# Layer 2 of a decode kernel: K and V in two places instead of three from unit 3 on, weights in the third, loop from unit 6

## The chip, the cores and the metric

The kernel runs on one core of a Trainium2 chip. The metric is the device time of one execution in microseconds.

## The reference

Two layers with the same weights. Each is an attention over a cache of 16384 keys for 2 batches and 32 heads, followed by a small MLP. There is one query row per batch.

```python
q = (x @ wq)                                              # x: (2, 1, 576), bf16
scores = einsum("bhqd,bhkd->bhqk", q, k_cache) * Dh**-0.5 # caches: (2, 32, 16384, 128)
o = einsum("bhqk,bhkd->bhqd", softmax(scores), v_cache)
x = x + o @ wo                                            # wo: (4096, 576)
...                                                       # mixer and MLP: w2, w3 (576 x 4608), w4 (4608 x 576)
```

The caches are 4 MB for each K and each V of one (batch, head). The kernel calls such a pair a *unit*; a layer has 64. Nearly all of K and V is read from memory twice, once per layer. That is about 1.1 GB, and it is the whole cost.

## The kernel before

A scheduler written in Python records operations with what they read and write, and derives the semaphore waits. One large buffer in SBUF, the memory on the chip, has three *places*, each with room for one K and one V. A queue of wishes says which tile goes where and in which order; a transfer is issued when everything that lies under its target has been read for the last time. The order of the queue is fixed: a tile that can't go yet holds up all behind it.

```python
def place(self, kind, l, i):              # l: layer (0, 1), i: unit in the layer
    if l == 0:
        return i % 2
    if kind == "K":
        return (0, 1, 2)[i % 3] if i < self.ROT else (2, 0)[i % 2]      # ROT = 8
    return (0, 1, 2)[i % 3] if i < self.ROT - 1 else (0, 2)[i % 2]

# in plan(): the order of the transfers in layer 2 (l = 1) is K2 V2 K3 V3 ... K6 V6 K7 K8 V7 wo K9 V8 ...
for l in range(2):
    wp = 2 - l                            # the place of this layer's weights: 2, then 1
    wo_at = wp * self.place_n + unit
    for i in range(U):
        kv("K", l, i, {(1, 2): (2, 1, 1), (1, 3): (2, 2)}.get((l, i)))  # split into several transfers
        ...
    want_w34(l, wp, 2)
```

Layer 1 uses places 0 and 1 for K and V and place 2 for weights. Its last two units are kept, so layer 2 starts with units 0 and 1 in SBUF, and with unit 2 as soon as the MLP has finished with place 2.

TensorE transposes 9 blocks of 16 of a unit's K and multiplies them by the query; VectorE does the other 7 blocks. TensorE then weighs V by the softmax. In the first units of layer 2 ("early") the weighing of the unit before is done in the middle of a unit, so that its V comes free sooner:

```python
first = (2, self.ROT)[l]                  # units from here on are one loop body of two units
self.s.loops.append((l * U + first, (U - first) // 2, 2, ...))
for i in range(U):
    early = l == 1 and 1 <= i < first
    for c in range(ncp):
        self.turn(l, i, c)                # TensorE transposes block c of K; ScalarE copies it
        ...
        if early and c == 4:
            self.weigh(l, i - 1, 0)
            self.weigh(l, i - 1, 1)       # V of unit i-1 is free from here on
    self.release("K", l, self.order[l][i], 1)
    if not early: ...                     # weigh at the end of the unit
```

I write K5 for the K of unit 5 of layer 2, and so on. All of this is about layer 2.

Of the kernel before, what the change touches and what calls it, by code (L numbers as in the profile page):

```python
# [278 lines left out]
class Decode:  # L279
# [3 lines left out]
    N_KEEP = 2  # L283
    N_MID = 3
    EARLY = 7
    ROT = 8
    WO_PIECE = 4
    FJ = 3
    W4_PIECES = ((1, 2, 3, 3, 2, 1), (5, 4, 2, 1))
# [89 lines left out]
        return ap[:, t * 128:(t + 1) * 128] if t < self.KT - 1 else ap[:, self.D - 128:self.D]  # L379


    def place(self, kind, l, i):


        if l == 0:
            return i % 2
        if kind == "K":
            return (0, 1, 2)[i % 3] if i < self.ROT else (2, 0)[i % 2]
        return (0, 1, 2)[i % 3] if i < self.ROT - 1 else (0, 2)[i % 2]

    def plan(self):
        ring, B, H, D, KT, U = self.ring, self.B, self.H, self.D, self.KT, self.U
        unit = 2 * self.half


        heads = [[*range(4, H), 0, 1, 2, 3], [*range(3, H - 1), 0, 1, 2, H - 1]]
        self.order = [[h * B + b for h in o for b in range(B)] for o in heads]
        x = self.order[0][0]
        assert self.order[1][:3] == [*self.order[0][-2:], x]
        self.kept = {(kind, u, h) for kind in "KV" for u in self.order[0][-2:] for h in range(2)} | {("V", x, 1)}  # L400

        def kv(kind, l, i, split=None):
            u = self.order[l][i]
            if l == 1 and (kind, u, 0) in self.kept:
                return
            b, hh = u % B, u // B
            src = {"K": self.K, "V": self.V}[kind][b, hh]
            pl = self.place(kind, l, i)
            at = pl * self.place_n + {"K": 0, "V": unit}[kind]
            ap = src.rearrange("(p j) d -> p (j d)", p=128)  # L410
            if split:
                a, quarter = 0, self.half // 2
                for k, n in enumerate(split):
                    if (kind, u) == ("V", x) and k == 1:
                        if l == 1:
                            continue
                        at = 2 * self.place_n + unit
                    part = ap[:, a * quarter:(a + n) * quarter]
                    ring.want([(kind, l, u, k)], at + a * quarter, n * quarter,
                              [lambda e, v, part=part: e.dma_start(v, part)])  # L420
                    a += n
            else:
                ring.want([(kind, l, u, h) for h in range(2)], at, unit, [lambda e, v: e.dma_start(v, ap)],
                          sem=f"{kind}{pl}")

        def rows(kind, l, w, ats):

            n = w.shape[1]
            for k in range(KT):
                if k < KT - 1:  # L430
                    ap, m = w[k * 128:(k + 1) * 128, :], n
                else:
                    m = n // 2
                    ap = w[k * 128:D, :].rearrange("r (c n) -> (r c) n", c=2)
                ring.want([(kind, l, k)], ats[k], m, [lambda e, v, ap=ap: e.dma_start(v, ap)])  # L435

        def want_w34(l, p, p1):
            base = p * self.place_n
            rows("w3", l, self.w3, [base + k * self.F for k in range(KT)])
            at, a0 = base + (2 * KT - 1) * self.F // 2, 0  # L440
            for c, n in enumerate(self.W4_PIECES[l]):
                m = n * self.FJ * D
                if c == 1:
                    assert at <= mid_at[l]
                    at = p1 * self.place_n
                ap = self.w4[a0 * 128 * self.FJ:(a0 + n) * 128 * self.FJ, :].rearrange(
                    "(a p j) n -> p a (j n)", p=128, j=self.FJ)
                ring.want([("w4", l, c)], at, m,
                          [lambda e, v, ap=ap, n=n: e.dma_start(v.rearrange("p (a m) -> p a m", a=n), ap)])
                at, a0 = at + m, a0 + n  # L450

        def want_w2(at):
            n = 128 * (KT - 1)
            w2a, w2b = self.w2[0:n, :].rearrange("(p r) n -> p (r n)", p=128), self.w2[n:D, :]
            ring.want([("w2",)], at, KT * D, [lambda e, v: e.dma_start(v[:, 0:(KT - 1) * D], w2a),
                                              lambda e, v: e.dma_start(v[0:64, (KT - 1) * D:KT * D], w2b)])

        def want_wo(l, j, at):
            h0, h1 = self.wo_piece(l, j)
            rows = self.wo[h0 * 128:h1 * 128, :]  # L460
            ap = rows.rearrange("(p j) n -> p j n", p=128) if j < self.n_wo else rows.rearrange("(j p) n -> p j n", p=128)
            ring.want([("wo", l, j)], at, (h1 - h0) * D,
                      [lambda e, v: e.dma_start(v.rearrange("p (j n) -> p j n", n=D), ap)],
                      sem="wo" if j < self.n_wo else None)

        n, third = self.wq.shape[1], 2 * self.place_n
        mid_at = [third + unit + self.half - self.N_MID * D, third - self.N_MID * D]
        rows("wq", 0, self.wq, [third + k * n for k in range(KT)])
        for l in range(2):
            wp = 2 - l  # L470
            wo_at = wp * self.place_n + unit
            for i in range(U):
                kv("K", l, i, {(1, 2): (2, 1, 1), (1, 3): (2, 2)}.get((l, i)))
                j = i if l == 1 and i < self.EARLY else i - 1
                if j >= 0 and (j != i - 1 or (l, j) != (1, self.EARLY - 1)):
                    kv("V", l, j, {(0, 0): (2, 2), (1, 2): (2, 2)}.get((l, j)))
                if i % 8 == 0 and 8 <= i <= 8 * self.n_wo:
                    want_wo(l, i // 8 - 1, wo_at)
                if i == 8 * self.n_wo + 2:
                    want_wo(l, self.n_wo, mid_at[l])  # L480
                if l == 0 and i == 0:
                    want_w2(wo_at + n // 2)
            kv("V", l, U - 1, (2, 1, 1))
            want_w34(l, wp, 2)
            if l == 0:
                free = third + (self.FA - self.W4_PIECES[0][0]) * self.FJ * D
                assert free + n <= third + unit + self.half
                rows("wq", 1, self.wq, [free, *(third + k * n for k in range(KT - 1))])
# [464 lines left out]
    def attention(self, l):  # L953
# [3 lines left out]
        self.query_rows(l, 0)  # L957
        first = (2, self.ROT)[l]
        self.s.loops.append((l * U + first, (U - first) // 2, 2, self.WO_PIECE, (9 - first) // 2 % self.WO_PIECE))
# [83 lines left out]
```

## Time and profile before

| | before |
|---|---|
| time | 2564.07 us (2563.78 to 2564.38, three runs) |
| span of the profiled run | 2562.7 us |
| data queue | 1095.66 MB, 99.7% of the span of 16 DMA engines |
| TensorE, VectorE, ScalarE busy | 65%, 68%, 48% |
| instruction packets of 16 KB | 40 |

In the lines of the profile PE is TensorE, PEld its weight loads, DVE VectorE, ACT ScalarE, POOL GpSimd, and SPq the queue of SyncE, which issues the transfers; L423 is line 423 of the kernel. From the page of the kernel before: the mean busy share of the DMA engines in 40 slices (9 is 90% or more), what they moved in each, and the queues (packets, MB, share of 16 engines).

```profile
...
DMA  9999999999999999999999999999999999999998
GB/s 409 430 431 433 431 430 433 432 431 432 430 433 432 431 432 431 433 431 431 426 408 431 428 432 430 432 433 431 432 432 430 432 431 431 433 432 431 430 433 341
...
q1 hardware_dynamic: 46888, 1095.66, 99.7%
q8 instruction: 40, 0.66, 0.1%
...
```

The queue is full in every slice but the last. The weaker slices are the first (409 GB/s), the two around the change of layers (426 and 408) and the last (341). The Trainium skill, page "DMA: Bandwidth & Descriptors", section Specifications, states a fabric ceiling of 435 GB/s, and the trace agrees: 428 to 433 in the slices between.

From the table of stretches of the kernel before (from and to in us from the span's start, length, busy us and count on each engine, then granted clock of TensorE, DMA share and GB/s):

```profile
...
core 0: us, PE busy (x) PEld busy (x) DVE busy (x) ACT busy (x) POOL busy (x), PEclk, DMA share, GB/s
...
1364.00:1368.00 4.00, 2.97 (x50) 2.98 (x51) 3.69 (x6) 1.51 (x2) 0.00 (x0) 0.50 1.01 434
1368.00:1372.00 4.00, 3.19 (x64) 2.95 (x62) 3.63 (x7) 3.31 (x6) 0.00 (x0) 0.91 0.94 397
1372.00:1378.00 6.00, 5.09 (x145) 4.55 (x144) 5.58 (x7) 4.79 (x9) 0.00 (x0) 1.00 1.03 436
1378.00:1384.00 6.00, 5.42 (x105) 5.42 (x105) 5.89 (x9) 3.41 (x5) 0.00 (x0) 0.58 1.02 434
1500.00:2480.00 980.00, 625.92 (x13949) 580.46 (x13946) 679.65 (x986) 474.27 (x750) 0.00 (x0) 0.67 1.00 431
...
```

In the stretch from 1364 to 1384 us the queue is full (0.94 to 1.03; a packet is counted whole in the stretch in which it starts, so a short stretch can show more than 1).

From the DMA queue's issues of the kernel before (start, length, line, target and source). They are V4, K5, V5 and K6:

```profile
...
start us, us, engine line op out<-in xcount [idle before <-releaser]
1347.50 0.33 SPq L423 DMA_DIRECT2D buf<-in_A_v_cache_dram  x1
1353.76 0.33 SPq L423 DMA_DIRECT2D buf<-in_A_k_cache_dram  x1
1365.57 0.33 SPq L423 DMA_DIRECT2D buf<-in_A_v_cache_dram  x1
1370.11 0.33 SPq L423 DMA_DIRECT2D buf<-in_A_k_cache_dram  x1
...
```

And what the DMA queue waited for between 1340 and 1385 us in the kernel before (L179 is the scheduler's own wait instruction, here for VectorE's reading of a K):

```profile
...
engine line waited for: us in total, times, longest us
SPq L423 <- PE ops L870: 29.4, 3, 11.5
SPq L179 <- DVE prod L827: 14.0, 3, 5.4
SPq L423 <- PE sps L815: 0.7, 1, 0.7
```

K5 goes at 1353.76 and V5 at 1365.57 us. When those transfers start matters less than when the one ahead has landed. Each of the 16 DMA engines reports its own landing; this is read from the trace's landing records:

| before | first engine | last engine | lag of the last |
|---|---|---|---|
| first half of K2 | 1316.5 | 1317.6 | 1.0 |
| V4 | 1365.3 | 1368.3 | 3.0 |
| K5 | 1375.0 | 1378.4 | 3.3 |
| V5 | 1384.7 | 1388.0 | 3.2 |
| V9 and all later ones of the loop | 1473.5 | 1479.7 | 6.2 |

A full tile of 4 MB takes 9.7 us. K5 was issued 11.5 us before V4's first engine had finished, V5 9.4 us before K5's: the queue has slack. And the slowest engine falls behind the fastest while unrolled code runs (until 1474 us), and then no more.

### The profile page before, as it was taken

The page shows a single profiled execution, that of the slowest core. Times are in us where ns is not written, and L with a number is a line of the kernel's source. Part 1 is how long each engine was busy: PE and PEld are TensorE (multiplying, and loading weights), DVE is VectorE, ACT ScalarE, POOL GpSimd, SP SyncE. Part 2 cuts the span into 40 slices and gives each one's busy share as a digit, 9 for nine tenths or more (in the row PEclk, how much of TensorE's full clock was granted, in tenths as well). Part 3 has the DMA queues.
Part 4 walks back from the last instruction along what each step waited for, and adds up shares of the span by engine and source line. Part 5 has one row for each costly group of instructions (what it writes and reads, how often), then busy time and mean ns, then how long its engine had stood idle before and what let it go on. Part 6 is the DMA issues. An engine that isn't in the chain of part 4 may idle for free.

```text
span 2562.7 us, 84020 instructions
## 1 busy us (share of the span) xinstructions
PE 1671.5 (65%) x36847; PEld 1559.0 (61%) x36847; DVE 1751.6 (68%) x2595; ACT 1231.3 (48%) x1944; POOL 1.0 (0%) x12
## 2 busy tenths in 40 slices
PE   5666666666666656666688766666656666665666
PEld 5555665565565656655678765565656555565566
DVE  5676767677666766766648777666767766676674
ACT  4544544454445445544446554454445544544452
POOL 0000000000000000000000000000000000000000
PEclk8666666666666666766666666666666666666665
DMA  9999999999999999999999999999999999999998
GB/s 409 430 431 433 431 430 433 432 431 432 430 433 432 431 432 431 433 431 431 426 408 431 428 432 430 432 433 431 432 432 430 432 431 431 433 432 431 430 433 341
DMA packets 46936, 1096.38 MB, mean 428 GB/s; under 512 B 4964, under 2 KB 6056, under 8 KB 11560
## 3 DMA queue, kind: packets, MB, share of 16 engines
q1 hardware_dynamic: 46888, 1095.66, 99.7%
q8 instruction: 40, 0.66, 0.1%
q14 instruction: 8, 0.07, 0.0%
HBM read 1095.64 MB, written 0.00 MB: 428 GB/s over the span
## 4 chain that ended last, share of the span: by engine, by line
DMA 59%; issue 16%; DVE 13%; PE 10%; ACT 1%; SPq 0%; DVEq 0%
DMA buf<-in_A_k_cache_dram 56%; DVE prod L827 11%; PE tps L798 6%; DMA buf<-in_B_w_dram 1%; DVE sd L830 1%; PE misc L846 1%; DMA buf<-in_A_v_cache_dram 1%; PE ops L870 1%; ACT ktsb L802 1%; PE misc L693 1%; DMA buf<-in_A_wq_dram 0%; PE sps L815 0%; SPq L435 0%; PE sps L655 0%; ACT p L856 0%
## 5 line engine op out<-in xcount | busy, mean ns | idle before, releaser
L802 ACT ACTIVATE ktsb<-tps 128x1024 bf16<-128x1024 bf16 x1155 | 1124.2, 1031 | 871.2 <-PE tps L798 866.2
L798 PE MATMUL tps<-ident,buf 128*128 128x128 bf16 x9240 | 911.7, 263 | 616.5 <-DMA buf<-in_A_k_cache_dram 600.4
L798 PEld LDWEIGHTS tps<-ident,buf 128*128 128x128 bf16 x9240 | 735.0, 120 | 643.1 <-DMA buf<-in_A_k_cache_dram 619.7
L830 DVE TENSOR_REDUCE sd<-prod 128x8 f32<-128x1024 bf16 x893 | 1089.5, 1220 | 31.0
L827 DVE TENSOR_TENSOR prod<-buf,qb 128x1024 bf16<-128x1024 bf16 x893 | 608.6, 682 | 11.4 <-DMA buf<-in_A_k_cache_dram 10.5
L870 PE MATMUL ops<-p,buf 128*128 128x1 bf16 x16384 | 461.7, 164 | 66.5 <-DMA buf<-in_A_v_cache_dram 57.4
L870 PEld LDWEIGHTS ops<-p,buf 128*128 128x128 bf16 x16384 | 443.7, 100 | 76.4 <-DMA buf<-in_A_v_cache_dram 66.4
L848 DVE TENSOR_REDUCE small<-misc 128x1 f32<-128x128 f32 x128 | 37.3, 292 | 635.8 <-PE misc L846 635.8
L815 PE MATMUL sps<-qcur,ktsb 128*128 128x1 bf16 x9240 | 396.8, 166 | 109.0 <-ACT ktsb L802 88.2
L815 PEld LDWEIGHTS sps<-qcur,ktsb 128*128 128x128 bf16 x9240 | 348.4, 101 | 172.2 <-ACT ktsb L802 166.1
L781 ACT ACTIVATE qb<-misc 128x128 bf16<-128x128 f32 x130 | 36.0, 277 | 369.2 <-PE misc L778 369.2
L846 PE MATMUL misc<-identS,small 128*128 128x128 f32 x256 | 94.4, 472 | 5.2 <-DVE small L840 5.2
L846 PEld LDWEIGHTS misc<-identS,small 128*128 128x128 f32 x256 | 69.7, 332 | 5.8 <-DVE small L840 5.7
L856 ACT ACTIVATE p<-sps,small 128x72 bf16<-128x72 f32 x128 | 41.4, 324 | 6.8 <-DVE small L848 6.8
L856 ACT ACTIVATE p<-sd,small 128x56 bf16<-128x56 f32 x128 | 44.6, 349 | 0.0
L773 ACT ACTIVATE qcur<-qt 128x1 bf16 (+1 forms) x130 | 29.4, 226 | 16.8 <-DVE qt L703 16.8
L778 PE MATMUL misc<-ident,qcur 128*128 128x128 bf16 x130 | 34.6, 266 | 1.3 <-ACT qcur L773 1.3
L925 PE MATMUL misc<-lpiece,small 128*128 128x16 f32 x28 | 8.5, 385 | 41.0 <-DVE lpiece L923 41.0
L925 PEld LDWEIGHTS misc<-lpiece,small 128*128 128x128 f32 x28 | 7.0, 311 | 43.6 <-DVE lpiece L923 43.6
L836 DVE TENSOR_REDUCE small<-sps 128x1 f32<-128x72 f32 x128 | 28.5, 223 | 4.1 <-PE sps L815 4.1
L693 PE MATMUL misc<-prod,buf 128*128 128x2 bf16 (+1 forms) x360 | 24.6, 179 | 6.6 <-DMA buf<-in_B_w_dram 4.6
L693 PEld LDWEIGHTS misc<-prod,buf 128*128 128x128 bf16 (+1 forms) x360 | 22.4, 111 | 8.8 <-issue 4.7
(94 smaller groups left out, 270.8 us busy)
## 6 DMA issues: line engine op xcount, KB each, us to landing
buf<-in_A_k_cache_dram SPq DMA_DIRECT2D x124, 4096.0 KB, 24.3
buf<-in_A_v_cache_dram SPq DMA_DIRECT2D x122, 4096.0 KB, 33.6
buf<-in_A_v_cache_dram SPq DMA_DIRECT2D x5, 2048.0 KB, 22.5
buf<-in_B_w_dram SPq DMA_DIRECT2D x8, 1152.0 KB, 30.7
buf<-in_A_wq_dram SPq DMA_DIRECT2D x8, 1024.0 KB, 9.0
buf<-in_A_wo_dram SPq DMA_DIRECT2D x14, 576.0 KB, 34.6
buf<-in_A_k_cache_dram SPq DMA_DIRECT2D x3, 2048.0 KB, 11.2
buf<-in_A_v_cache_dram SPq DMA_DIRECT2D x4, 1024.0 KB, 23.8
```

The lines of the kernel that those rows point to most:

```text
L693: ins = pe.matmul(out[lo:128, t * self.B:(t + 1) * self.B], lhsT=w[:, t * 128:(t + 1) * 128 - lo], rhs=rhs, start=(first and t == 0), stop ...
L778: self.pe(lambda pe: pe.matmul(self.misc[:, 0:128], lhsT=bcast(self.qcur[:, q:q + 1], 128), rhs=self.ident[:, :], start=True, stop=True), ...
L781: self.act(lambda a: a.activation(out=self.qb[q][:, :], in_=self.misc[:, 0:128], func=ACT.Copy), r=["P:misc"], w=[f"qb{q}"])
L798: ins = pe.transpose(self.tps[b][:, j * 128:(j + 1) * 128], kt[:, (j0 + j) * 128:(j0 + j + 1) * 128], self.ident[:, :])
L802: self.act(lambda a: a.activation(out=self.ktsb[k][:, :, :].rearrange("p a b -> p (a b)"), in_=self.tps[b][:, :], func=ACT.Copy), r=[f"P:t ...
L815: ins = pe.matmul(self.sps[sp][:, col:col + 1], lhsT=self.ktsb[k][:, j, :], rhs=self.qcur[:, sp:sp + 1], start=True, stop=True)
L827: self.dve(lambda v: v.tensor_tensor(out=self.prod[d][:, :, :], in0=k3, in1=bcast_mid(self.qb[q][:, :], self.CH), op=ALU.mult), r=[*res, f ...
L830: self.dve(lambda v: v.tensor_reduce(out=self.sd[q][:, o:o + self.CH], in_=self.prod[d][:, :, :], axis=AX.X, op=ALU.add), r=[f"prod{d}"], ...
L846: self.pe(lambda pe: pe.matmul(self.misc[:, 128:256], lhsT=bcast(self.m[:, q:q + 1], 128), rhs=self.identS[:, :], start=True, stop=True), ...
L848: self.dve(lambda v: v.tensor_reduce(out=self.bias[:, q:q + 1], in_=self.misc[:, 128:256], axis=AX.X, op=ALU.max, negate=True), r=["P:misc ...
L856: self.act(lambda a, u, c0=c0, c1=c1, src=src: a.activation(out=self.p[q][:, c0:c1], in_=src, func=ACT.Exp, bias=self.bias[:, q:q + 1], sc ...
L870: ins = pe.matmul(self.ops[q][:, 0:1], lhsT=vt[:, j * 128:(j + 1) * 128], rhs=self.p[q][:, h * self.TB + j:h * self.TB + j + 1], start=(h ...
```

## The change

It gives up the third place for K and V after unit 2, so that weights can lie there in both layers, and with the shorter pattern the loop of layer 2 can start at unit 6 instead of 8, which is less code. K5 is split in two halves so that its first half can go as soon as K3's first half is free.

```diff
-    ROT = 8
+    ROT = 6
...
-    def place(self, kind, l, i):
-        if l == 0:
-            return i % 2
-        if kind == "K":
-            return (0, 1, 2)[i % 3] if i < self.ROT else (2, 0)[i % 2]
-        return (0, 1, 2)[i % 3] if i < self.ROT - 1 else (0, 2)[i % 2]
+    def place(self, l, i):
+        if l == 0 or i < 3:
+            return i % 2 if l == 0 else i
+        return (i + 1) % 2
...
         for l in range(2):
-            wp = 2 - l
-            wo_at = wp * self.place_n + unit
+            wo_at = third + unit
             for i in range(U):
-                kv("K", l, i, {(1, 2): (2, 1, 1), (1, 3): (2, 2)}.get((l, i)))
+                kv("K", l, i, {(1, 2): (2, 1, 1), (1, 3): (2, 2), (1, 5): (2, 2)}.get((l, i)))
...
-            want_w34(l, wp, 2)
+            want_w34(l, 2, 2 - l)
```

The cut parts only rename the argument of `place` and move the address of a weight tile.

More of the change, by code (lines that the diff above doesn't have):

```diff
@@ L407, in kv @@
             src = {"K": self.K, "V": self.V}[kind][b, hh]
-            pl = self.place(kind, l, i)
+            pl = self.place(l, i)
             at = pl * self.place_n + {"K": 0, "V": unit}[kind]
@@ L466, in plan @@
         n, third = self.wq.shape[1], 2 * self.place_n
-        mid_at = [third + unit + self.half - self.N_MID * D, third - self.N_MID * D]
+        mid_at = [third + unit + self.half - self.N_MID * D, third + self.place_n - self.N_MID * D]
         rows("wq", 0, self.wq, [third + k * n for k in range(KT)])
         for l in range(2):
-            wp = 2 - l
-            wo_at = wp * self.place_n + unit
+            wo_at = third + unit
             for i in range(U):
-                kv("K", l, i, {(1, 2): (2, 1, 1), (1, 3): (2, 2)}.get((l, i)))
+                kv("K", l, i, {(1, 2): (2, 1, 1), (1, 3): (2, 2), (1, 5): (2, 2)}.get((l, i)))
                 j = i if l == 1 and i < self.EARLY else i - 1
```

## The prediction

> **What bounds it now.** The transfers. The page's DMA line is full in every slice but the last; one queue takes 99.7% of the 16 engines' span for 1095.66 MB. The stretch table gives 431 GB/s in both layers' loops. The Trainium skill ("DMA: Bandwidth & Descriptors", Specifications) gives a fabric ceiling of 435 GB/s; the trace agrees with it and not with that table's 358 GB/s per core. PE (65%) and DVE (68%) have slack: in the loop PE waits some 5.7 us per unit for K. So only bubbles in the transfers, and what the slowest of the 16 engines loses, can move the time.
>
> **What the change does.** Layer 1, layer 2's first units, all bytes, the steady loop (two places in both kernels) and the end stay. Between about 1310 and 1480 us three things move.
>
> 1. In layer 2, K5 waits for unit 3 instead of unit 2, V5 for V3 instead of V2, and so on: one place less of prefetch while compute catches up after the MLP. K5 is split; its first half waits only for the first half of K3.
> 2. Units 6 and 7 move from unrolled code into the loop, so V5 and V6 come free later in their units.
> 3. Two unrolled units less code. The trace has some 23 instruction fetches of 16 KB between 1313 and 1474 us, two per unrolled unit, about 1 us each on one DMA engine. Meanwhile the gap between the first and the last engine's landing of one tile grows from 1.0 to 6.2 us, and stays there.
>
> **Costed from the landings and issues.** V4 lands from 1365.3 (first engine) to 1368.3 us (last). Before, K5 was issued at 1353.8, V5 at 1365.6: no bubble. Now K5's first half can go only when unit 3's eighth block of transposes is done, about 1368.5; at layer 2's first K the first packet came 0.96 us after issue, and first packets took about 1.1 us instead of 0.61. So the queue runs dry: about 1.9 us lost on the slowest engine, 4.9 on the fastest. K5 then lands about 1380; V5 goes at 1379.6 (V3 done): another 1.2 us. K6 (free 1384.5), V6 (1393.6), K7 (1399.8), K8 (about 1416) go before the queue empties. Sum +3.1 us, all critical, since transfers bound the kernel to its end.
>
> In return, four or five fetches fewer: the slowest engine lost 2.9 us to them from 1388 to 1480; I estimate 1 us saved. PE, ACT and DVE work is the same and off the path.
>
> **Prediction:** 2564.1 + 3.1 - 1.0 = about 2566.2 us, 8 in 10 between 2562.8 and 2569.0. Faster by over 2%: 0.003; within 2%: 0.99; slower by over 2%: 0.007.
>
> **What would show it right.** Stretch table: a new dip of DMA share at about 1366 to 1371, a small one at 1380 to 1382; V5 landing 2 to 3 us later than 1388.0; the loop still at 431 GB/s; the same 8 us from the last landing to the end. The DMA queue's waits: K5's first half on PE's transposes, V5 on PE's weighting. Some four instruction packets fewer (40 before), and a gap between first and last landing in the loop below 6.2 us.
>
> **What would make it wrong.** If K5's first half goes before V4 has drained, no bubble, and the saved fetches win: about 2563. If the loop's first pass (units 6, 7) is slow, K8 and K9 slip and more bubbles appear: 2569 or more. If the slow engine's lag is not what ends the kernel, the cost is nearer the 4.9 us of the fast ones.

## The result and the profile after

The changed kernel took 2567.89 us (median of 2565.89, 2566.49, 2569.29 and 2569.38) against 2563.93 us of the kernel before in the same rounds. The ratio is 1.0015, with a 95% interval of 0.9998 to 1.0032: the same at 2%. A ratio is the mean time of one kernel's runs over that of the other's of the same rounds, so it is not quite the ratio of the medians. The first repetition below gave 1.0019 (1.0005 to 1.0033). Over all nine runs the changed kernel has a mean of 2568.2 us, 4.3 us above the 2563.9 us of before. Its runs lie 4.0 us apart, those of before 1.5.

The profile is that of the fastest run (2565.89 us, span 2564.1 us). The same lines of its page:

```profile
...
DMA  9999999999999999999999999999999999999998
GB/s 410 432 428 433 432 432 430 432 433 431 431 431 430 432 433 429 433 433 432 424 411 404 431 431 431 432 431 432 430 431 431 432 430 433 431 431 432 430 432 351
...
q1 hardware_dynamic: 47032, 1095.66, 99.6%
q8 instruction: 35, 0.57, 0.1%
...
```

Slice 22 (of 64 us each, so from 1346 us on) has 404 instead of 431 GB/s, and there are 35 instruction packets instead of 40. The bytes are the same.

The same stretches of the changed kernel:

```profile
...
core 0: us, PE busy (x) PEld busy (x) DVE busy (x) ACT busy (x) POOL busy (x), PEclk, DMA share, GB/s
...
1364.00:1368.00 4.00, 3.74 (x68) 3.56 (x65) 3.93 (x7) 3.59 (x5) 0.00 (x0) 0.66 0.46 135
1368.00:1372.00 4.00, 3.03 (x44) 2.80 (x45) 3.04 (x7) 2.67 (x5) 0.00 (x0) 0.77 0.89 377
1372.00:1378.00 6.00, 6.00 (x174) 6.00 (x172) 5.86 (x8) 3.45 (x7) 0.00 (x0) 0.78 0.97 408
1378.00:1384.00 6.00, 4.81 (x91) 4.46 (x88) 5.89 (x8) 5.07 (x7) 0.00 (x0) 0.80 1.04 401
1500.00:2480.00 980.00, 627.84 (x13954) 583.39 (x13954) 679.54 (x985) 474.44 (x749) 0.00 (x0) 0.67 1.00 431
...
```

Between 1364 and 1368 us the DMA share falls from 1.01 to 0.46, and at 1378 to 1384 the rate falls from 434 to 401 GB/s. The loop (last row) is unchanged. So are TensorE's and VectorE's work; before, they were as busy as now.

The same issues (V4, then the two halves of K5 in one row, V5, K6):

```profile
...
1346.07 0.33 SPq L421 DMA_DIRECT2D buf<-in_A_v_cache_dram  x1
1366.49 2.44 SPq L418 DMA_DIRECT2D buf<-in_A_k_cache_dram  x2
1377.32 0.33 SPq L421 DMA_DIRECT2D buf<-in_A_v_cache_dram  x1
1383.28 0.33 SPq L421 DMA_DIRECT2D buf<-in_A_k_cache_dram  x1
...
```

And the same waits of the DMA queue. The wait of 20.3 us is that of K5's first half, which by the program is for unit 3's eighth block of transposes; the profile puts it down to the matmuls (`sps`) among which that block is issued. `ops` is the weighing of V, where V5 waits for V3:

```profile
...
SPq L418 <- PE sps L812: 20.3, 1, 20.3
SPq L421 <- PE ops L867: 17.2, 2, 8.8
...
```

K5 went 12.7 us later than before, and V5 11.8 us later. V4 had landed at 1364.9 (first engine) to 1367.4 us (last), so the queue ran dry. V5 landed at 1390.7 instead of 1388.0 us. In the loop the lag of the slowest engine is 3.2 us instead of 6.2. The last transfer landed at 2555.9 us, 1.4 us later than before, and from there to the end the kernels take 8.1 and 8.2 us.

### The profile page after: what moved, and what is told of

It reads as the page before. It is cut to its first block, busy times and chain, and to the rows that moved or that the text cites. A ratio compares the mean times of both kernels' runs of the same rounds, so it can differ in the third digit from the quotient of the medians.

```text
span 2564.1 us, 84103 instructions
## 1 busy us (share of the span) xinstructions
PE 1663.0 (65%) x36847; PEld 1544.4 (60%) x36847; DVE 1751.5 (68%) x2595; ACT 1228.4 (48%) x1944; POOL 1.0 (0%) x12
## 4 chain that ended last, share of the span: by engine, by line
DMA 59%; issue 16%; DVE 15%; PE 8%; ACT 1%; SPq 0%; DVEq 0%
DMA buf<-in_A_k_cache_dram 56%; DVE prod L824 12%; PE tps L795 5%; DVE sd L827 2%; DMA buf<-in_B_w_dram 2%; PE misc L843 1%; DMA buf<-in_A_v_cache_dram 1%; PE misc L690 1%; ACT ktsb L799 1%; PE ops L867 1%; DMA buf<-in_A_wq_dram 0%; SPq L433 0%; DVE small L845 0%; PE sps L652 0%; PE sps L812 0%
## 5 line engine op out<-in xcount | busy, mean ns | idle before, releaser
L795 PE MATMUL tps<-ident,buf 128*128 128x128 bf16 x9240 | 896.1, 260 | 621.4 <-DMA buf<-in_A_k_cache_dram 605.5
L795 PEld LDWEIGHTS tps<-ident,buf 128*128 128x128 bf16 x9240 | 722.1, 119 | 647.4 <-DMA buf<-in_A_k_cache_dram 625.0
```

The lines of the kernel that those rows point to most:

```text
L795: ins = pe.transpose(self.tps[b][:, j * 128:(j + 1) * 128], kt[:, (j0 + j) * 128:(j0 + j + 1) * 128], self.ident[:, :])
```

## The experiments

Two theories were put against each other. *The hole*: K5 and V5 wait for a unit more, the queue runs dry, and a kernel that is bound by transfers never gets that back, except for what the saved instruction fetches return. *The loop*: units 6 and 7 moved into the loop free their V later and start with a cold first pass, and that is what costs. All runs gave the right result. Each was timed in five rounds beside the kernel before, whose median was between 2563.90 and 2564.01 us in each of the three sets. The sets ran on three chips; since before is equal on them, medians of different sets are compared here.

### The changed kernel again

No edit.

> The changed kernel again, unedited, to see whether its two groups of times (2565.9 and 2566.5; 2569.3 and 2569.4 us) come back. Theory (the bubble at K5 and V5 plus the fetches that are saved): times between 2565.5 and 2570 us, in two groups or spread; if this profile is of a long run (2569 us), K5's first half is issued later than the 1366.5 us of the first profile, by 2 to 3 us, or the lag of the slowest engine in the loop is above 3.2 us; which of the two tells where the 3 us lie. Rival (the loop's first pass over units 6 and 7 costs the time): the bubble is the same in both groups and K8 or K9 comes late instead.

Measured: 2568.4 us (2567.31 to 2569.87), ratio 1.0019 (1.0005 to 1.0033). The two groups did not come back; the times are spread. The profiled run took 2568.40 us. Its K5 (both halves) and V5:

```profile
...
1368.35 1.86 SPq L418 DMA_DIRECT2D buf<-in_A_k_cache_dram  x2
1379.21 0.33 SPq L421 DMA_DIRECT2D buf<-in_A_v_cache_dram  x1
...
```

and its stretches:

```profile
...
1364.00:1368.00 4.00, 3.20 (x52) 3.20 (x53) 3.90 (x7) 1.74 (x2) 0.00 (x0) 0.50 0.19 78
1368.00:1372.00 4.00, 3.20 (x64) 2.95 (x63) 3.44 (x6) 3.31 (x6) 0.00 (x0) 0.94 0.69 233
...
```

K5 went 1.9 us later than in the first profile of the same kernel, V5 too, and the run was 2.5 us longer. The hole is deeper: a DMA share of 0.19 from 1364 to 1368 us. So in these two profiles the longer run is the one with the longer hole, and compute was through unit 3 later in it by as much: unit 4's query comes at 1370.6 instead of 1368.7 us. That the other runs differ for the same reason is likely but not shown, as they were not profiled.

### The loop put back to unit 8

```diff
 # the changed kernel
-    ROT = 6
+    ROT = 8
```

> The changed kernel with the loop put back to unit 8 (units 6 and 7 unrolled and early again); the two places stay. Theory: the bubble stays (K5 and V5 wait as in the changed kernel), the fetches come back (about 40 packets), so it is slower than the changed kernel by about 1 us: 2567 to 2570.5 us. Rival (the earlier loop is what costs): as fast as before, 2564 us, since the loop is undone.

Measured: 2569.69 us (2568.79 to 2570.35), ratio 1.0023 (1.0009 to 1.0036), 40 instruction packets. The loop is undone and the time is 1.3 us longer than in the repetition, not 4.5 us shorter. The theory of the loop falls.

### Three places up to unit 5, loop from unit 6

```diff
 # the kernel before
-    ROT = 8
+    ROT = 6
 ...
-        if kind == "K":
-            return (0, 1, 2)[i % 3] if i < self.ROT else (2, 0)[i % 2]
-        return (0, 1, 2)[i % 3] if i < self.ROT - 1 else (0, 2)[i % 2]
+        return i % 3 if i < self.ROT else (0, 2)[i % 2]
 ...
-            want_w34(l, wp, 2)
+            want_w34(l, wp, (2, 0)[l])
```

> Three places up to unit 5 as in the kernel before (so K5 waits for unit 2 again, V5 for V2), two places after, loop from unit 6 as in the changed kernel. Theory: no bubble, about 35 instruction packets, lag of the slowest engine in the loop about 4.5 to 5.5 us instead of 6.2: 2562.3 to 2563.5 us, faster than both by 0.5 us or more. Rival (the earlier loop costs): about as slow as the changed kernel, 2566 to 2568 us. A third reading, that fetches cost nothing: 2563.9 us, as before.

Measured: 2563.61 us (2562.85 to 2564.27), ratio 0.9999 (0.9985 to 1.0013), 35 instruction packets. Its stretches:

```profile
...
1364.00:1368.00 4.00, 3.02 (x51) 3.03 (x52) 3.93 (x7) 1.56 (x2) 0.00 (x0) 0.50 1.01 434
1368.00:1372.00 4.00, 3.12 (x63) 2.78 (x61) 3.83 (x7) 3.31 (x6) 0.00 (x0) 0.90 0.94 397
1372.00:1378.00 6.00, 5.14 (x145) 4.74 (x145) 5.39 (x7) 4.74 (x9) 0.00 (x0) 1.00 1.03 436
1378.00:1384.00 6.00, 5.21 (x99) 5.21 (x100) 5.90 (x9) 3.19 (x5) 0.00 (x0) 0.59 0.99 423
...
```

The holes are gone, and with them the whole loss, while the loop is as early as in the changed kernel. That puts the loss on the places from unit 5 on and not on the loop. This edit also lets K6 and V6 go one unit sooner than in the changed kernel, leaves K5 whole and puts the weights elsewhere; but in the changed kernel K6 was issued 5.5 us before V5's first landing and V6 6.9 us before K6's, so these two were not late; splitting K5 is tested next; and in the table at the end both placements of the weights take 1173.4 to 1173.8 us after V5. The gain from the saved fetches is smaller than expected: 0.3 us by the medians. One reason is a new, small hole that I had overlooked when I wrote the edit: K8 now lies in K6's place and goes only when unit 6 is done, at about 1414.5 us, when the first engine had already landed K7 (1413.85 us).

### K5 in one piece

```diff
 # the changed kernel
-                kv("K", l, i, {(1, 2): (2, 1, 1), (1, 3): (2, 2), (1, 5): (2, 2)}.get((l, i)))
+                kv("K", l, i, {(1, 2): (2, 1, 1), (1, 3): (2, 2)}.get((l, i)))
```

> The changed kernel with K5 loaded in one piece, so it waits for all of unit 3, VectorE's last product included. Theory: K5 is issued about 1.6 to 2.5 us later than in the changed kernel, the bubble grows by that, and nothing hides it: 2568 to 2571 us, spread in the profile's stretch 1364 to 1372 us deeper. Rival (the loop costs): no difference from the changed kernel.

Measured: 2568.99 us (2567.09 to 2571.13), ratio 1.0022 (1.0008 to 1.0036). The range held, but the reason I gave for it did not: K5 was issued at 1369.47 us, 1.1 us later than in the repetition above, and the run grew by only 0.6 us. V5 went at 1379.66 us (1379.21 in the repetition), with K5 in the queue until 1382.8 us (1382.0 in the repetition), and landed only 0.4 us later. So most of K5's further delay did not reach V5. V5 was issued 1.4 us before the first engine was done with K5 (1381.04 us) and yet landed 10.7 us after K5, 1.0 more than a tile takes: an issue just ahead of the drain did not keep the queue whole.

### K5 alone back in the third place

```diff
 # the changed kernel
-            pl = self.place(l, i)
+            pl = 2 if (kind, l, i) == ("K", 1, 5) else self.place(l, i)
 # and K5 in one piece, as above
```

> The changed kernel with K5 alone put back in the third place, in one piece; V5 and all later tiles stay in two places, loop from unit 6. Theory: the first hole (1364 to 1369 us) is gone, V5 still waits for V3 at about 1379.5 us while K5 lands at about 1375 to 1378.5 us, so one hole of 1.5 to 3 us is left: 2565 to 2567 us, between e2 (2563.6) and the changed kernel (2568.4). Rival (the loop, or V freed late in units 6 and 7): as the changed kernel.

Measured: 2568.77 us (2567.24 to 2569.85), ratio 1.0018 (1.0005 to 1.0032). This was a miss: K5's hole is gone and the time is that of the changed kernel. Its issues of K5 and V5:

```profile
...
1353.90 0.33 SPq L421 DMA_DIRECT2D buf<-in_A_k_cache_dram  x1
1378.95 0.33 SPq L421 DMA_DIRECT2D buf<-in_A_v_cache_dram  x1
...
```

and its stretches:

```profile
...
1364.00:1368.00 4.00, 3.10 (x52) 3.11 (x53) 3.93 (x6) 1.64 (x2) 0.00 (x0) 0.50 1.01 434
1368.00:1372.00 4.00, 3.29 (x63) 3.20 (x62) 3.50 (x7) 3.27 (x6) 0.00 (x0) 0.83 0.95 406
1372.00:1378.00 6.00, 5.31 (x149) 4.67 (x149) 5.66 (x7) 4.81 (x9) 0.00 (x0) 0.85 0.53 223
1378.00:1384.00 6.00, 5.39 (x105) 5.30 (x104) 5.90 (x9) 4.08 (x5) 0.00 (x0) 0.58 0.73 265
...
```

K5 goes at 1353.90 us as in the kernel before, and from 1364 to 1368 us the queue is full. But V5 still waits for V3 until 1378.95 us, and now nothing is in the queue ahead of it: the hole has moved to 1372 to 1384 us (shares of 0.53 and 0.73). V5 landed at 1392.4 us, only 0.7 us earlier than in the repetition with both waits. That is 13.5 us after its issue; in the two profiles of the changed kernel it is 13.4 and 13.9 us. So once V5 has to wait for V3, K5's wait adds 0 to 0.5 us.

### V5 alone in the third place

This could only be done on the kernel with the loop from unit 8, because a V5 that is read inside the loop has to lie where V7 lies.

```diff
 # the changed kernel with ROT = 8
-            pl = self.place(l, i)
+            pl = 2 if (kind, l, i) == ("V", 1, 5) else self.place(l, i)
```

> The kernel of e1 (two places, loop from unit 8) with V5 alone in the third place (in e1, since a V5 that is read inside the loop can't lie apart). In e6 K5's hole was taken away and V5's hole took its place (V5 landed 13.7 us after K5, at 1392.4 us, as late as with both holes): so the two waits seem to be two bounds of which the later counts, not a sum. If so, V5 alone leaves K5's bound: K5 lands at about 1382 us, V5 about 10 us later, 1391.7 to 1392.3 us instead of 1392.9 in e1; the run takes 2568 to 2569.5 us, at most 1.5 us under e1 (2569.7). If the two waits add up, as the prediction summed them, taking V5's away gives 1.2 us or more on its own and e6 should have gained the rest, which it did not. If V5's wait is the only bound that counts: 2564 to 2565.5 us.

Measured: 2568.05 us (2566.06 to 2568.63), ratio 1.0016 (1.0003 to 1.0030), which is 1.6 us under the kernel that it edits. The two halves of K5, and V5:

```profile
...
1366.87 1.88 SPq L418 DMA_DIRECT2D buf<-in_A_k_cache_dram  x2
1368.79 0.44 SPq L421 DMA_DIRECT2D buf<-in_A_v_cache_dram  x1
...
```

V5 follows K5 without a wait of its own, and K5's hole is left. By the criterion (1.2 us or more if the two waits add up, at most 1.5 us if not) the gain of 1.6 us speaks for a sum, and the forecast of V5's landing (1391.7 to 1392.3 us) was a miss: it landed at 1390.1 us. But the profiled run had an early K5, issued 1.8 us sooner than in the profile of the kernel that it edits (1366.87 against 1368.71 us), so times alone do not decide. Counted from K5's issue, V5 landed after 23.3 us here, after 24.1 us in the kernel that it edits, and after 24.2 and 24.8 us in the two profiles of the changed kernel. So V5's wait, which comes last in the queue, adds 0.9 to 1.5 us to what K5's wait costs, and taking it away gives that back. Taking away K5's wait gives back 0 to 0.7 us, because V5's wait then ends about as late as before. V5's loss was 2.7 and 5.2 us; only the kernel with both tiles in the third place returns it all. The two waits are two bounds on the same queue: what one of them costs depends on whether the other is there.

### 32 idle matmuls ahead of unit 2, in both kernels

```diff
             for c in range(ncp):
+                if (l, i, c) == (1, 2, 0):
+                    def idle(pe):
+                        for _ in range(32):
+                            ins = pe.matmul(self.misc[:, 0:128], lhsT=self.ident[:, :], rhs=self.ident[:, :],
+                                            start=True, stop=True)
+                        return ins
+                    self.pe(idle, r=["ident"], w=["P:misc"])
                 self.turn(l, i, c)
```

In the changed kernel:

> The changed kernel with 32 idle 128x128 matmuls put ahead of unit 2 of layer 2 (TensorE work that nobody reads; results stay right). At the transposes' 0.06 to 0.11 us each they take 2 to 3.5 us. Theory: in the changed kernel the queue is dry until unit 3's transposes are done, so TensorE's time up to there is on the critical path: +1.5 to +3.5 us on the changed kernel, 2570 to 2572 us. Rival (the time is set by the loop or the fetches): no difference, 2568.4 us.

In the kernel before:

> The same 32 idle matmuls in the kernel before. Theory: there K5 is issued some 11 us and V5 some 9 us before their turn in the queue, so 2 to 3.5 us more of TensorE change nothing: 2563.5 to 2564.5 us. If TensorE's pace mattered in itself: 2566 us or more.

Measured: 2569.41 us (2567.36 to 2571.35), ratio 1.0023 (1.0009 to 1.0037), for the changed kernel, and 2564.49 us (2563.74 to 2566.42), ratio 1.0003 (0.9990 to 1.0017), for the kernel before. The first is a miss: +1.0 us by the medians instead of 1.5 to 3.5. The load made unit 2 longer by about 3 us (18.1 us from query to query, 15.1 to 15.7 in the other profiles of this placement), but unit 3 then took 14.0 us instead of 15.4 in the repetition (14.2 to 15.8 in the other profiles), and V5 was issued at 1380.05 us, only 0.8 us later than in the repetition. The difference between the two kernels, 1.0 against 0.5 us, is too small beside their scatter to show anything. This pair is inconclusive.

### The kernel before with the loop from unit 16

```diff
 # the kernel before; places and order of work stay
-        self.s.loops.append((l * U + first, (U - first) // 2, 2, self.WO_PIECE, (9 - first) // 2 % self.WO_PIECE))
+        loop = (2, 16)[l]
+        self.s.loops.append((l * U + loop, (U - loop) // 2, 2, self.WO_PIECE, (9 - loop) // 2 % self.WO_PIECE))
```

> The kernel before with the loop of layer 2 started at unit 16 instead of 8: same places, same order of work, eight more unrolled units, so some 16 more instruction packets (about 56 instead of 40). If a fetch costs the slowest DMA engine what e1 against the changed kernel shows (0.9 to 1.3 us for 5 packets, 0.2 to 0.25 each), +3 to +4.5 us: 2567 to 2568.5 us, and the lag of the slowest engine in the loop grows from 6.2 to 9 us or more. If fetches cost nothing: 2564 us. If they cost only in a queue that has just been aligned by a hole: under +2 us.

Measured: 2567.22 us (2567.05 to 2567.67), ratio 1.0014 (1.0000 to 1.0028). The queues on its page:

```profile
...
q1 hardware_dynamic: 46888, 1095.66, 99.6%
q8 instruction: 57, 0.93, 0.1%
...
```

There are 17 more packets of 16 KB (57 instead of 40), and the median is 3.3 us above that of before (2563.90), so about 0.2 us per packet. The lag of the slowest engine in the loop is 8.3 us instead of 6.2, and the last transfer landed at 2557.3 us instead of 2554.5. 17 packets of 16 KB are 0.28 MB, which at 431 GB/s would be 0.65 us if they were spread over 16 engines; they cost five times that. No hole explains it: from 1483 to 1640 us, where the added code runs, the first engine keeps landing a tile every 9.7 us, while the last falls back from 5.2 to 8.3 us behind it, and it stops falling back after the last of these packets (1626 us). The lag expected was 9 us or more, so this part was a miss.

### The first wo piece ahead of K8

This fills the new hole of the kernel with three places to unit 5.

```diff
 # the kernel with three places to unit 5
             for i in range(U):
+                if (l, i) == (1, 8):
+                    want_wo(l, 0, wo_at)
                 kv("K", l, i, ...)
 ...
-                if i % 8 == 0 and 8 <= i <= 8 * self.n_wo:
+                if i % 8 == 0 and 8 <= i <= 8 * self.n_wo and (l, i) != (1, 8):
```

> The kernel of e2 (three places to unit 5, loop from unit 6) with the first wo piece of layer 2 (0.6 MB, about 1.4 us of transfer) put ahead of K8 in the queue. In e2's profile K8 waits for unit 6 until 1414.9 us while the first engine has drained at 1413.85; K8 landed 10.86 us after K7 instead of 9.72, so 1.1 us were lost there. Theory: the wo piece fills that hole, K8's landing plus wo's comes 11.1 to 11.3 us after K7's, and the run takes 2562.0 to 2563.0 us, about 0.5 to 1 us under e2 and 1 to 1.5 us under before. If engines' lag is all that counts: no gain, 2563.5 us.

> The kernel of e5 again, for its distance from before (0.55 us by the medians, inside the interval): if it is real, 2563.0 to 2563.7 us against 2563.9 to 2564.1 us. If it was luck of the rounds: no difference.

Measured: 2563.43 us (2562.90 to 2564.07), ratio 0.9998 (0.9984 to 1.0012), and in the second set 2563.07 us (2562.89 to 2563.67), ratio 0.9998 (0.9984 to 1.0011). The wo piece and K8 together landed 11.1 us after K7, as expected, so what the slowest engine lost there is won back. The gain in time was less than expected (2562.0 to 2563.0 us; the second set held its range), and the slowest engine lags more in the loop: 5.0 and 3.5 us in the two profiles, 2.5 us in that of the kernel without this edit. A hole lets the slowest engine catch up (in the changed kernel the lag was 2.4 us at V4 and 0.4 us at K5's first half); what the filled hole gives the fastest engines is not all time gained. The means are 0.55 and 0.58 us below those of the kernel before in the two sets. This is the fastest version found, but both intervals include 1, so it is not shown to be faster than before.

### All profiles in one table

K5 and V5 issued, V5's last landing, the lag in the loop, the span of the profiled run (all from the traces, us), the instruction packets, and what is left after V5, which is the span less V5's landing:

| | K5 issued | V5 issued | V5 landed | lag in loop | packets | span | after V5 |
|---|---|---|---|---|---|---|---|
| before | 1353.8 | 1365.6 | 1388.0 | 6.2 | 40 | 2562.7 | 1174.7 |
| before, idle matmuls | 1358.3 | 1368.2 | 1388.3 | 5.1 | 40 | 2562.3 | 1174.0 |
| three places to unit 5 | 1354.8 | 1365.5 | 1388.3 | 2.5 | 35 | 2561.8 | 1173.5 |
| the same, wo first (first profile) | 1352.3 | 1364.0 | 1387.8 | 5.0 | 35 | 2561.6 | 1173.8 |
| V5 alone in the third place | 1366.9 | 1368.8 | 1390.1 | 3.5 | 40 | 2563.9 | 1173.8 |
| changed, first profile | 1366.5 | 1377.3 | 1390.7 | 3.2 | 35 | 2564.1 | 1173.4 |
| K5 alone in the third place | 1353.9 | 1379.0 | 1392.4 | 2.2 | 35 | 2566.0 | 1173.6 |
| changed, second profile | 1368.4 | 1379.2 | 1393.2 | 3.7 | 35 | 2566.6 | 1173.4 |
| changed, loop from 8 | 1368.7 | 1379.4 | 1392.9 | 3.6 | 40 | 2566.7 | 1173.8 |
| changed, idle matmuls | 1368.1 | 1380.1 | 1393.5 | 1.9 | 35 | 2567.2 | 1173.7 |
| changed, K5 whole | 1369.5 | 1379.7 | 1393.6 | 2.7 | 35 | 2567.2 | 1173.6 |
| before, loop from 16 | 1353.7 | 1365.3 | 1387.6 | 8.3 | 57 | 2565.4 | 1177.8 |

The span follows V5's landing. What comes after it goes with the number of instruction packets: 1173.4 to 1173.8 us with 35 (mean of seven 1173.6), 1173.8 to 1174.7 with 40 (mean of four 1174.1), 1177.8 with 57. So what happens up to V5 is the loss, and the five saved packets return about 0.5 us after it; the groups of 35 and 40 touch at 1173.8, so this figure is rough. The lag of the slowest engine in the loop is no measure of that: it is smaller after a hole, since the fast engines waited too.

## Why the prediction was right or wrong

The time, 2567.9 us, lies within the range, 1.7 us above the point. The direction and the mechanism were right; the term for K5's hole was too small. The interval of the first rounds reaches below 1 (from 0.9998), that of the repetition does not (from 1.0005).

- *Transfers bind to the end.* Right. The loop ran at 431 GB/s in both kernels, 8.1 to 8.2 us passed from the last landing to the end in both, and every delay of V5 came out at the end of the run.
- *K5 and V5 wait, and the queue runs dry from about 1366 to 1371 us, then a little at 1380.* Right in place and cause: the waits on unit 3's transposes and on V3's weighing are there, and the version with both tiles in the third place has no loss. In the first profile K5 came 2 us earlier than forecast, since compute was ahead of the profile before; in the repetition it was issued at 1368.35 us, as forecast (1368.5).
- *"about 1.9 us lost on the slowest engine".* Too small; this is the term that was most off. K5's last landing came 12.7 us after V4's in the first profile and 14.4 in the second, where 9.7 is the time of the tile: 3.0 and 4.7 us lost. I let the slowest engine restart level with the others and stay level. It restarted nearly level (a lag of 0.4 and 0.6 us at K5's first half), but was 1.9 and 2.0 us behind at the end of the second half. Instruction packets passed in that time (at 1373.9 and 1378.2 us in the first profile, at 1375.8 us in the second) and may have set one engine back; that this is the cause was not tested. The split is not the cause: with K5 whole the lag at its end was 1.8 us. Put in another way, the prediction gave a tile that finds the queue dry 11.5 us from its issue to its last landing (K5 1368.5 to about 1380); K5 took 13.6 and 13.7 us, and V5 in the kernel with K5 alone in the third place 13.5.
- *"another 1.2 us" for V5, "Sum +3.1 us".* V5's own loss was 0.9 and 1.4 us, as predicted. The sum holds when it is read along the queue, as K5's loss and then what V5's wait adds; it does not say what each wait costs alone. Taking away V5's wait returned its term, but taking away K5's returned 0 to 0.7 us and not 1.9 or 3. V5 landed 2.7 us late in the first profile and 5.2 in the second, where 3.1 was predicted. That the first comes close is partly luck: K5 lost 1.1 us more than forecast, but V4 had landed 1.0 us earlier than in the kernel before.
- *Four or five fetches fewer, 1 us saved.* Five, right. They return about 0.5 us by the table, and 1.3 us by the medians of the changed kernel with the loop from 8 and from 6, where the scatter is larger. My estimate lies between. The dose of 17 packets gave 0.2 us each.
- *K6 to K8 go in time, the loop's first pass costs nothing.* Right: with the loop put back the time rose, and K6, V6, K7 and K8 were issued 2.9 to 10.6 us before the first engine had landed the tile ahead.
- *Not foreseen: the scatter.* The hole lasts until compute is through unit 3, and the changed kernel's runs lie 4.0 us apart, those of before, which has slack there, 1.5. In the profile of the fastest run TensorE's granted clock from 1312 to 1340 us was 0.81, in that of the repetition 0.72. The Trainium skill, page "TensorE: Matmul & The Clock Gate", section "What's actually happening", says that the window that sets this clock is free-running and that the phase varies from run to run; the profiles agree with that in so far as two runs of the same kernel show different clocks. The two other profiles in which K5 is split and no work was added fit in: V5 alone in the third place 0.74 and K5 issued at 1366.9 us, loop from 8 0.68 and 1368.7 us. That this clock makes the scatter is argued from these four profiles; the idle matmuls, meant to show that compute's pace sets the time, did not settle it.

## What to carry to other kernels

In a kernel bound by transfers, don't count bytes or engine time; take the tile whose buffer comes free latest, compare the moment when it may be issued with the moment when the queue ahead of it drains, and look at the next tile too: two late tiles are two bounds, and mending one leaves the other (here 0 to 0.7 us gained of 5.2 by mending K5 alone). An issue just ahead of the drain may not be enough: V5 in the kernel with K5 whole went 1.4 us ahead and lost 1.0 us, K8 in the changed kernel went 2.9 us ahead and lost nothing (one profile each). Less prefetch cost time here where compute was catching up after the MLP had held the buffers; in the steady loop both kernels have two places, and these were enough (431 GB/s). Unrolled code was not free either: 17 more instruction packets cost 3.3 us.

## What the Trainium skill lacked or had wrong

- "Runtime: NRT & Kernel Launch", section "Instruction fetch mechanics", states that crossing a 16 KiB boundary of the code is "mostly hidden". It does not say what a fetch costs the data transfers: in this kernel, whose data queue is full, 17 more packets of 16 KB cost 3.3 us, about 0.2 us each. The page's remark that kernels prefer full unrolling has this exception.
- "DMA: Bandwidth & Descriptors", section Specifications, gives about 0.6 us to the first byte of a transfer issued from SyncE and does not say from which moment. In the trace of before, the first packet of layer 2's first K came 0.96 us after the start of its issue, which took 0.33 us: 0.63 from the end of the issue agrees. The first packets then took about 1.1 us instead of 0.61, which the page does not tell.
- No page tells that the 16 engines of one queue drift apart while code is fetched and stay apart: the last landing of a tile came 1.0 us after the first at 1317 us, 6.2 us in the loop of the kernel before, 8.3 us with eight more units unrolled.
